# A fused attention and two-layer kernel: the first layer's weights are loaded from ScalarE's queue

## The chip, the cores and the metric

One core of a Trainium2 chip runs the whole program. The metric is the device time of one execution in microseconds (us). The engines are PE (TensorE, matmuls; PEld are its weight loads), DVE (VectorE), ACT (ScalarE), POOL (GpSimd) and SP (SyncE, which here only begins transfers). Each engine works through its own list of instructions in order, and an instruction that waits on a semaphore holds everything behind it on that engine.

## The reference

```python
q_pool = q.reshape(B, H, S // 2, 2, D).mean(axis=3)          # B 4, H 8, S 1152, D 64
scores = q_pool @ k.transpose(0, 1, 3, 2) / sqrt(D)
attn = exp(scores - max(scores)); attn = attn / sum(attn)
x = (attn @ v) as 2304 rows of 512
h = x @ moe_w_in;  x = (h * cos(h)) @ moe_w_out               # 512 to 2048 to 512, weights float64
h = x @ moe2_w_in; out = (h / (1 + exp(-h))) @ moe2_w_out     # the same shapes
```

All inputs and the output are taken as the reference has them: the attention inputs are float32, and the kernel has a way (`wide`) of reading weights whose numbers are eight bytes long.

## The kernel before

The work is cut into 16 pairs of heads: 4 batches, and in each 4 pairs. For a pair, `pair_loads` (L289) begins the transfers of q, k and v, `pair_prep` (L313) finds their largest values (L111, tiles `pm`), makes a scale `ps` from them (L102) and splits each number into a high and a low float16 (L351, L352, L306, L311), and two transposing transfers turn q and k (L357 `qT`, L367 `kT`). A pair has 9 tiles of 128 query rows. Each tile runs `tile_scores` (PE, L391, into the PSUM tiles `sp`), `tile_exp` (DVE L410 reads the scores and their largest value, L415, then ACT L418), `tile_hi` (ACT L424), `tile_lo` (POOL L429, then the transposing transfer `hlT` of L431, 144 of them in the program) and, four tiles later, `tile_pv` (PE, L442 and L446).

The weights of the first layer, `W1`, come in 16 pieces of 1 MB, 8 of `w_in` and 8 of `w_out`, through three buffers named `wst`. `weight_steps` (L155) runs them: `more` (L172) begins a piece's transfer (L177), `decode` (L191) turns the eight-byte numbers into float32 with one ACT instruction (L206, absolute values into `wt`) and four of DVE (L207, L210, L215, L218, of 1024 columns each), then a scale is made as for a pair (L87, L90, L95, L98, L102, L106), and `write` (L232) splits the piece into two float16 halves (ACT L238 and L239, POOL L240) and calls `more` again, which refills the buffer that L240 has just read. The engine that begins the transfers is an argument, `eng`. Three pieces are requested when the generator starts; 13 refills follow.

The second layer's weights, `W2`, go through the same function late in the program (from 925 us in the profile on). The first layer's matmuls (L522, L582) begin after the first batch and run beside the attention of the others; the second layer's (L522, L603) run last, alone.

The order in which the instructions stand on each engine isn't written by hand. The framework places them from the program's order, priorities (`ahead`, `early`) and its own model of when each could run. Each transfer takes the next of eight completion semaphores (DMAHW0 to DMAHW7, in turns over all queues) and waits until that semaphore's last transfer has landed. So a change of a queue moves instructions on every engine.

Of the kernel before, what the change touches and what calls it, by code (L numbers as in the profile page):

```python
# [29 lines left out]
W1_SUB, W1_BUFS, W1_AHEAD, WT_BUFS = 1, 3, 1, 2  # L30
# [14 lines left out]
def attention_moe_moe_kernel(ctx, tc, q, k, v, w_in1, w_out1, w_in2, w_out2, out):  # L45
# [3 lines left out]
    nc = tc.nc  # L49
# [14 lines left out]
    ps_h = ctx.enter_context(tc.tile_pool(name="ps_h", bufs=2, space=PSUM))  # L64
# [56 lines left out]
    def early(g, n):  # L121
        while True:
            with ahead(n):
                r = next(g, END)
            if r is END:
                return
            yield r

    def run_all(g):
        for _ in g:  # L130
            pass
# [13 lines left out]
    def new_w(tag, npc):  # L145
        w = Weights()
        w.npc = npc
        for nm in ("si", "ui", "so", "uo"):
            setattr(w, nm, const.tile([128, npc], F32, name=nm + tag))
        w.uoT = const.tile([128, NC], F32, name="uoT" + tag)  # L150
        w.kg = const.tile([128, 1], F32, name="kg" + tag)
        w.ug = const.tile([128, 1], F32, name="ug" + tag)
        return w
# [122 lines left out]
    def pair_new(at, b, j):  # L276

        P = Pair()  # L280
        P.b, P.j = b, j
        P.on_pool = PREP_POOL if b == 0 else 0
        P.q = at.src.tile([128, 2 * NT + 1, 2, D], F32, tag="stq", name="stq", bufs=1)
        P.k, P.v = (
            [at.src.tile([128, KC, D], F32, tag="stg", name="st" + nm, bufs=NB_S) for i in range(2)] for nm in "kv"
        )
        return P

    def pair_loads(P):  # L289
        heads = (P.j, P.j + NP)  # L290
        n = NT * 128 * 2
        for i, h in enumerate(heads):
            nc.sync.dma_start(
                out=P.q[:, i * NT:(i + 1) * NT], in_=q[P.b, h, 0:n, :].rearrange("(p t r) d -> p t r d", t=NT, r=2)
            )
            nc.sync.dma_start(
                out=P.q[i * 64:(i + 1) * 64, 2 * NT], in_=q[P.b, h, n:, :].rearrange("(p r) d -> p r d", r=2)
            )
            yield
        for src, t in ((k, P.k), (v, P.v)):  # L300
            for i, h in enumerate(heads):
                nc.sync.dma_start(out=t[i], in_=src[P.b, h].rearrange("(p c) d -> p c d", c=KC))
                yield
# [316 lines left out]
    if True:  # L620
        W1 = new_w("1", 8)
# [7 lines left out]
        wst = wst_stack.enter_context(tc.tile_pool(name="wst", bufs=1, reuse_waits="tile"))  # L629
# [66 lines left out]
        for n in range(2):  # L696
            P[n] = pair_new(at, *pairs[n])
            run_all(pair_loads(P[n]))
            if n == 0:
                wg = weight_steps(W1, (w_in1, w_out1), wst, lambda: ps_h, nc.sync, W1_SUB, W1_BUFS, W1_AHEAD)  # L700
                next(wg)
                run_all(pair_prep(at, P[0]))

        def slowly(g, n):
            for _ in g:
                for _ in range(n):
                    yield

        wg = early(slowly(wg, W_PACE), P_W)
# [265 lines left out]
```

## Time and profile before

| | us |
|---|---|
| median of 3 runs | 1421.21 (1418.97 to 1424.5) |
| the profiled execution | 1422.36 |
| its span, first to last instruction | 1420.6 |
| PE busy | 1159.3, 82% |
| DVE busy | 994.6, 70% |
| ACT busy | 774.0, 54% |
| POOL busy | 568.2, 40% |

The shares are averages over stages that differ. A table of busy time by stretch shows a first stage to about 213 us in which DVE is hardly ever idle, a middle one to about 1030 us in which PE and DVE are both between some 75 and 90%, and a last one, to the end, in which PE alone is full. Such a row gives, after the stretch and its length, each engine's busy time with the number of its instructions, then TensorE's granted clock as a share of full speed, the busy share of the 16 DMA engines, and GB/s. In rows of a timeline the columns are start, duration, engine, line, operation, output and inputs, shapes and count; in brackets stands how long the engine was idle just before, and what ended that.

### The profile page before, as it was taken

To read this page: it belongs to the slowest core of one execution; us is meant where nothing else is said; L and a number is where in the kernel's file an instruction comes from. 1 tells how busy PE (TensorE), PEld (TensorE's weight loads), DVE (VectorE), ACT (ScalarE), POOL (GpSimd) and SP (SyncE) were. 2 spreads that over 40 slices of the span, in tenths; PEclk is the share of its full clock that TensorE was granted. 3 is DMA by queue.
4 is the path that set the end of the run, shared out by engine and by line. 5 is a ranking of instruction groups with operands and counts; after the bars stand their busy time and mean duration, and the time that the engine had idled before them with its cause. 6 is when DMAs were issued, how large, how long until landed. Compare 5 with 4: busy or idle time off the path is not lost. (4 is left out here: it accounts for less than half of the span.)

```text
span 1420.6 us, 25141 instructions
## 1 busy us (share of the span) xinstructions
PE 1159.3 (82%) x10020; PEld 850.6 (60%) x10020; DVE 994.6 (70%) x1944; ACT 774.0 (54%) x955; POOL 568.2 (40%) x312
## 2 busy tenths in 40 slices
PE   1465356688888778889889889888799999999998
PEld 0243233476676556667667668677686666666664
DVE  7999997689777898878998976999932322323221
ACT  3686587578677778867779585556611111111110
POOL 1577366545666466645666453354510000000000
PEclk9976578898999989999999999999999999999999
DMA  7799779987799999978999964433210000000000
GB/s 230 191 237 213 184 157 207 204 169 133 143 210 174 204 183 220 191 142 171 177 205 178 201 121 106 123 113 104 75 60 30 23 8 30 30 30 16 16 5 27
DMA packets 493334, 186.19 MB, mean 131 GB/s; under 512 B 433312, under 2 KB 468128, under 8 KB 493216
## 3 DMA queue, kind: packets, MB, share of 16 engines
q1 hardware_dynamic: 493216, 184.59, 61.6%
q8 instruction: 78, 1.28, 0.4%
q14 instruction: 40, 0.33, 0.1%
HBM read 66.58 MB, written 9.44 MB: 54 GB/s over the span
## 5 line engine op out<-in xcount | busy, mean ns | idle before, releaser
L429 POOL TENSOR_TENSOR hl<-sc,hl 128x1152 f16<-128x1152 f32 x144 | 365.5, 2548 | 201.7 <-ACT hl L424 111.7
L391 PE MATMUL sp<-kT,qT 128*128 128x512 f16 (+1 forms) x768 | 191.7, 366 | 111.5 <-DVE sc L410 84.1
L522 PEld LDWEIGHTS <-ih 128*128 128x128 f16 x2304 | 227.4, 100 | 69.0 <-issue 9.7
L535 ACT ACTIVATE hk<-h,ca 128x512 f32<-128x512 f32 x144 | 98.0, 682 | 313.0 <-PE h L522 311.2
L410 DVE TENSOR_SCALAR_CACHE_REDUCE sc<-sp,psu 128x512 f32<-128x512 f32 (+1 forms) x288 | 229.3, 807 | 46.4 <-PE sp L391 40.4
L418 ACT ACTIVATE sc<-sc,nb 128x1152 f32<-128x1152 f32 x144 | 179.8, 1250 | 94.1 <-DVE nb L415 81.1
L442 PE MATMUL pv<-vt,hlT 128*128 128x130 f16 (+1 forms) x1440 | 192.3, 236 | 39.7 <-DMA hlT<-hl 30.7
L522 PE MATMUL h<-ys,ih 128*128 128x256 f16 x1152 | 196.2, 273 | 1.8 <-ACT hk L535 1.8
L522 PE MATMUL h<-xT,ih 128*128 128x256 f16 x1024 | 192.3, 282 | 6.3 <-ACT hk L535 3.1
L442 PEld LDWEIGHTS <-hlT 128*128 128x128 f16 (+1 forms) x1440 | 145.2, 109 | 70.0 <-DMA hlT<-hl 42.7
L446 PE MATMUL pv<-vt,hlT 128*128 128x65 f16 (+1 forms) x1440 | 184.4, 206 | 0.0
L391 PEld LDWEIGHTS <-qT 128*128 128x128 f16 x768 | 76.7, 108 | 174.0 <-issue 130.5
L424 ACT ACTIVATE hl<-sc 128x1152 f16<-128x1152 f32 x144 | 165.2, 1155 | 21.6 <-DMA hlT<-hl 10.8
L570 DVE TENSOR_SCALAR gh<-hk,ck 128x1024 f16<-128x1024 f32 x36 | 27.0, 751 | 207.5 <-PE o L603 193.7
L582 PE MATMUL y<-gh,oh 128*128 128x256 f16 x576 | 159.7, 277 | 4.8 <-ACT y L591 4.8
L582 PE MATMUL y<-gl,oh 128*128 128x256 f16 x576 | 159.7, 277 | 1.5 <-POOL gl L563 1.5
L582 PE MATMUL y<-gh,ol 128*128 128x256 f16 x576 | 159.7, 277 | 0.0
L522 PE MATMUL h<-ys,il 128*128 128x256 f16 x576 | 157.0, 273 | 0.0
L446 PEld LDWEIGHTS <-hlT 128*128 128x128 f16 (+1 forms) x1440 | 140.7, 107 | 15.0 <-issue 6.2
L522 PE MATMUL h<-xT,il 128*128 128x256 f16 x512 | 144.1, 281 | 0.0
L582 PEld LDWEIGHTS <-oh 128*128 128x128 f16 x1152 | 113.8, 100 | 24.5 <-issue 7.4
L522 PEld LDWEIGHTS <-il 128*128 128x128 f16 x1152 | 114.7, 100 | 19.2 <-issue 2.7
(284 smaller groups left out, 2048.6 us busy)
## 6 DMA issues: line engine op xcount, KB each, us to landing
stk<-in_k_dram SPq DMA_DIRECT2D x32, 288.0 KB, 4.1
stv<-in_v_dram SPq DMA_DIRECT2D x32, 288.0 KB, 4.4
stq<-in_q_dram SPq DMA_DIRECT2D x32, 256.0 KB, 3.1
wst<-in_moe_w_in_dram SPq DMA_DIRECT2D x8, 1024.0 KB, 5.9
wst<-in_moe_w_out_dram SPq DMA_DIRECT2D x8, 1024.0 KB, 6.2
wst<-in_moe_w_in_dram SPq DMA_DIRECT2D x16, 512.0 KB, 4.5
wst<-in_moe_w_out_dram SPq DMA_DIRECT2D x16, 512.0 KB, 4.7
ydr<-y SPq DMA_DIRECT2D x9, 512.0 KB, 3.0
```

Of the source, the lines that this page charges most:

```text
L391: nc.tensor.matmul(sp[:, o - a:o - a + n], P.qT[e][:, t, :], kT[:, o:o + n], start=(e == 0), stop=(e == 1))
L410: nc.vector.tensor_scalar(out=T.sc[:, a:z], in0=sp, scalar1=T.P.su, scalar2=None, op0=ALU.mult, op1=ALU.min, accum_out=mx[:, x:x + 1],)
L418: nc.scalar.activation(out=T.sc, in_=T.sc, func=AF.Exp, scale=-1.0, bias=nb)
L424: nc.scalar.activation(out=hi, in_=T.sc, func=AF.Copy)
L429: nc.gpsimd.tensor_tensor(out=T.hl[:, 1, :], in0=T.sc, in1=T.hl[:, 0, :], op=ALU.subtract)
L442: nc.tensor.matmul(G.pv[r, T.gi], T.hlT[:, 0, c, r], P.vt[i][:, c], start=(c == 0), stop=(c == KC - 1), skip_group_check=True,)
L446: nc.tensor.matmul(G.pv[r, T.gi, 0], T.hlT[:, 1, c, r], P.vt[i][:, c, 0], start=False, stop=(c == KC - 1), skip_group_check=True,)
L522: nc.tensor.matmul(hp, wt[:, c, f * 128:(f + 1) * 128], xt(c), start=(i == 0), stop=(i == 3 * NC - 1), skip_group_check=True,)
L535: nc.scalar.activation(out=o, in_=blk.hp, func=AF.Copy if first else AF.Silu, scale=blk.c.a[:, g:g + 1])
L570: nc.vector.tensor_scalar(out=gh, in0=hk, scalar1=blk.c.k, scalar2=None, op0=ALU.mult)
L582: nc.tensor.matmul(blk.y[:, oc, :], wt[:, f, oc * 128:(oc + 1) * 128], gt[:, f % 4, :], start=(f == 0 and e == 0 and oc % 2 == 0), stop=(f ...
```

## The change

The generator of `W1` is given ScalarE's queue in place of SyncE's. All 16 transfers of L177 for `W1` stand on ACT now; the 16 and 16 smaller ones of `W2` and all others stay on SP.

```diff
             if n == 0:
-                wg = weight_steps(W1, (w_in1, w_out1), wst, lambda: ps_h, nc.sync, W1_SUB, W1_BUFS, W1_AHEAD)
+                wg = weight_steps(W1, (w_in1, w_out1), wst, lambda: ps_h, nc.scalar, W1_SUB, W1_BUFS, W1_AHEAD)
                 next(wg)
```

The start of ACT's list, before. `qn`, `kn` and `vt` are the split q, k and v of the first pair, `wst_132`, `wst_134` and `wst_136` the first three weight pieces:

```order
L351 ACT_TABLE_LOAD [waits DMAHW1_49,DMAHW2_49,DMAHW0_49,DMAHW3_49,DVE_49]
L351 ACTIVATE qn_157<-stq_119,ps__148 128x9x64 [waits Pool_49]
L351 ACTIVATE qn_157<-stq_119,ps__148 128x9x64
L306 ACTIVATE kn_164<-stk_120,ps__148 128x9x64 [waits DMAHW4_49]
L306 ACTIVATE kn_164<-stk_121,ps__148 128x9x64 [waits DMAHW5_49]
L306 ACTIVATE vt_171<-stv_122,ps__148 128x9x64 [waits DMAHW6_49]
L306 ACTIVATE vt_176<-stv_123,ps__148 128x9x64 [waits DMAHW7_49]
L206 ACTIVATE wt_215<-wst_132 128x1024 [waits DMAHW0_49]
L206 ACTIVATE wt_234<-wst_134 128x1024 [waits DMAHW1_49]
L206 ACTIVATE wt_276<-wst_136 128x1024 [waits DMAHW2_49,DVE_49]
```

and now:

```order
L177 DMA wst_132<-in_moe_w_in_dram 128x4x512
L177 DMA wst_134<-in_moe_w_in_dram 128x4x512
L177 DMA wst_136<-in_moe_w_in_dram 128x4x512
L206 ACT_TABLE_LOAD
L206 ACTIVATE wt_215<-wst_132 128x1024 [waits DMAHW0_49]
L206 ACTIVATE wt_234<-wst_134 128x1024 [waits DMAHW3_49]
L206 ACTIVATE wt_276<-wst_136 128x1024 [waits DMAHW5_49,DVE_49]
L351 ACTIVATE qn_157<-stq_119,ps__148 128x9x64 [waits DMAHW2_49,DMAHW4_49,DMAHW1_49,DMAHW6_49,DVE_49,Pool_49]
L351 ACTIVATE qn_157<-stq_119,ps__148 128x9x64
L306 ACTIVATE kn_164<-stk_120,ps__148 128x9x64 [waits DMAHW7_49]
```

The three transfers and the three weight instructions L206 have moved ahead of the first pair's instructions.

DVE's list around the first scores (L410 reads `sp`), before:

```order
L90 SCALAR_TENSOR_TENSOR mw_224<-wm_214,mw_224 128x1 [waits DVE_49]
L215 SCALAR_TENSOR_TENSOR wst_134<-wst_134,wt_234 128x1024 [waits DMAHW1_49,DVE_49]
L90 SCALAR_TENSOR_TENSOR mw_261<-wm_233,mw_261 128x1 [waits DVE_49]
L218 SCALAR_TENSOR_TENSOR wst_132<-wst_132 128x1024 [waits DVE_49]
L98 TENSOR_SCALAR ui1_75<-bm_227 128x1 [waits PE_49]
L207 TENSOR_SCALAR wt_276,wm_275<-wt_276 128x1024 [waits Activation_49]
L218 SCALAR_TENSOR_TENSOR wst_134<-wst_134 128x1024 [waits DVE_49]
L98 TENSOR_SCALAR ui1_75<-bm_264 128x1 [waits PE_49]
L102 TENSOR_SCALAR si1_74<-ui1_75 128x1 [waits DVE_49]
L410 TENSOR_SCALAR sc_202,mx_203<-sp_194,psu_155 128x512 [waits PE_49]
```

and now:

```order
L102 TENSOR_SCALAR si1_74<-ui1_75 128x1 [waits DVE_49]
L355 COPY qn_157<-qn_157 128x9x64 [waits DVE_49]
L106 TENSOR_SCALAR ui1_75<-ui1_75 128x1 [waits DVE_49]
L311 SCALAR_TENSOR_TENSOR kn_164<-stk_120,ps__148,kn_164 128x9x64 [waits Activation_49]
L311 SCALAR_TENSOR_TENSOR kn_164<-stk_121,ps__148,kn_164 128x9x64 [waits Activation_49]
L311 SCALAR_TENSOR_TENSOR vt_171<-stv_122,ps__148,vt_171 128x9x64 [waits Activation_49]
L311 SCALAR_TENSOR_TENSOR vt_176<-stv_123,ps__148,vt_176 128x9x64 [waits Activation_49]
L410 TENSOR_SCALAR sc_202,mx_203<-sp_194,psu_155 128x512 [waits PE_49]
L410 TENSOR_SCALAR sc_202,mx_203<-sp_195,psu_155 128x640 [waits PE_49]
L111 TENSOR_REDUCE pm_220<-stk_183 128x1 [waits DMAHW2_49]
L410 TENSOR_SCALAR sc_246,mx_247<-sp_238,psu_155 128x512 [waits PE_49]
L415 TENSOR_SCALAR nb_206<-mx_203 128x1 [waits DVE_49]
```

All three pieces are decoded ahead of the first pair's split now (in before the third piece's L210, L215 and L218 stand behind the first L410), and nothing stands between the split of v (`vt`) and the first L410. Up to the first L410 the list has one L210, one L215, one L218 and eight instructions of 1 to 3 columns more than before. From the fourth L207 on the two lists have the weights and the score tiles in nearly the same mixture; from the 535th of DVE's 1610 instructions (376 us in the profile of before) to the 1254th they are alike, row for row.

ACT's list in the middle of the first stage, before. `oh` is the high half of a piece of `w_out`, L206 opens the next piece:

```order
L239 ACTIVATE wst_650<-wst_650,so1_76 128x1024 [waits Activation_49]
L206 ACTIVATE wt_867<-wst_802 128x1024 [waits DMAHW0_49]
L238 ACTIVATE oh1_83<-wst_728,so1_76 128x16x64 [waits DVE_49]
L239 ACTIVATE wst_728<-wst_728,so1_76 128x1024 [waits Activation_49,Pool_49]
L465 ACTIVATE x32_575<-pvs_1515,den_1512 128x64 [waits DVE_49]
L465 ACTIVATE x32_576<-pvs_1515,den_1512 128x64 x2
L238 ACTIVATE oh1_83<-wst_802,so1_76 128x16x64 [waits DVE_49]
```

and now:

```order
L238 ACTIVATE oh1_83<-wst_650,so1_76 128x16x64 [waits DVE_49]
L177 DMA wst_802<-in_moe_w_out_dram 128x16x128 [waits Pool_49]
L239 ACTIVATE wst_650<-wst_650,so1_76 128x1024 [waits Activation_49]
L238 ACTIVATE oh1_83<-wst_728,so1_76 128x16x64 [waits DVE_49]
L206 ACTIVATE wt_867<-wst_802 128x1024 [waits DMAHW1_49]
L177 DMA wst_863<-in_moe_w_out_dram 128x16x128 [waits Pool_49]
L239 ACTIVATE wst_728<-wst_728,so1_76 128x1024 [waits Activation_49]
L177 DMA wst_923<-in_moe_w_out_dram 128x16x128 [waits Pool_49]
L206 ACTIVATE wt_933<-wst_863 128x1024 [waits DMAHW3_49]
```

Each refill stands on ACT behind the L239 of some piece and waits on POOL's L240; where two follow each other closely, as here, ACT's L206 for the next piece stands behind them. On SP the refills are gone, and the pair's loads and transposes follow each other.

Before the third pair's first L410 DVE's list has the same shape: behind the split of k (`kn`) stand the split of v and two weight pieces' instructions, of L207 one fewer than before.

## Rows read from the trace of the kernel before

**Rows 1.** Busy time by stretch: us, PE, PEld, DVE, ACT, POOL, clock, DMA share, GB/s.

```profile
0.00:35.50 35.50, 5.94 (x18) 2.92 (x18) 25.26 (x52) 13.28 (x14) 5.55 (x15) 1.00 0.78 230
...
71.00:106.50 35.50, 21.95 (x186) 14.69 (x185) 35.35 (x77) 29.47 (x32) 25.52 (x12) 0.71 1.11 237
...
35.50:213.00 177.50, 88.21 (x688) 57.61 (x688) 172.32 (x345) 123.40 (x136) 105.78 (x52) 0.73 0.89 196
213.00:284.00 71.00, 46.04 (x437) 29.77 (x438) 48.66 (x129) 46.74 (x54) 43.00 (x25) 0.84 1.09 206
...
960.00:1030.00 70.00, 57.36 (x488) 48.99 (x488) 66.68 (x130) 43.68 (x68) 34.45 (x20) 0.95 0.30 91
```

**Rows 2.** DVE's timeline, start of the program to the first scores.

```profile
7.27 0.75 DVE L111 TENSOR_REDUCE pm<-stk 128x1 f32<-128x576 f32 x1 [6.27 <-DMA stk<-in_k_dram]
...
12.30 0.17 DVE L102 TENSOR_SCALAR ps__148<-pu__149 128x3 int32<-128x3 int32 x1
...
18.98 1.22 DVE L207 TENSOR_SCALAR_CACHE_REDUCE wt<-wt 128x1024 f32<-128x1024 f32 x1
...
22.59 0.68 DVE L210 TENSOR_SCALAR wt<-wt 128x1024 int32<-128x1024 int32 x1
...
23.26 1.22 DVE L215 SCALAR_TENSOR_TENSOR wst<-wst,wt 128x1024 int32<-128x1024 int32 x1
...
25.66 1.22 DVE L218 SCALAR_TENSOR_TENSOR wst<-wst 128x1024 int32<-128x1024 int32 x1
...
29.58 0.74 DVE L410 TENSOR_SCALAR_CACHE_REDUCE sc<-sp,psu 128x512 f32<-128x512 f32 x1
```

**Rows 3.** Timelines of SP, ACT and PE in the same stretch.

```profile
0.74 0.40 SPq L293 DMA_DIRECT2D stq<-in_q_dram  x1
...
16.06 3.94 SPq L357 DMA_TRANSPOSE qT<-qn  x1
20.11 2.69 SPq L367 DMA_TRANSPOSE kT<-kn  x1
...
12.54 1.28 ACT L351 ACT_TABLE_LOAD   x1 [12.54 <-DVE ps__148 L102]
...
17.84 2.13 ACT L206 ACTIVATE wt<-wst 128x1024 f32<-128x1024 f32 x2
...
26.25 2.08 PE L391 MATMUL sp<-kT,qT 128*128 128x512 f16 x6
```

**Rows 4.** Weight pieces, issue to landing: the first three, then all 16 of `W1`.

```profile
DMA to landing us min/median/max: 8.1/10.3/12.4
...
DMA to landing us min/median/max: 5.2/6.1/12.4
```

**Rows 5.** Instructions on the tile `wst` to 213 us: ns min/median/max, first and last start.

```profile
L177 SPq DMA_DIRECT2D wst<-in_moe_w_out_dram x8: 367/523/692, 93.4 to 178.5; - x8
...
L240 POOL TENSOR_TENSOR il<-wst,ih x8: 2129/2224/3109, 32.2 to 118.8; 128x1024 f16<-128x1024 f32 x8
```

**Rows 6.** The transposing transfers of L431 to 213 us, in the same columns.

```profile
L431 SPq DMA_TRANSPOSE hlT<-hl x24: 2486/2782/5341, 44.4 to 202.1; - x24
```

**Rows 7.** DVE's groups by shape to 376 us: busy us, mean ns | idle before.

```profile
L215 DVE SCALAR_TENSOR_TENSOR wst<-wst,wt 128x1024 int32<-128x1024 int32 x16 | 30.4, 1898 | 0.0
L218 DVE SCALAR_TENSOR_TENSOR wst<-wst 128x1024 int32<-128x1024 int32 x16 | 27.7, 1729 | 0.0
L210 DVE TENSOR_SCALAR wt<-wt 128x1024 int32<-128x1024 int32 x16 | 21.0, 1313 | 0.0
```

**Rows 8.** DVE's waits from 213 to 284 us: total, times, longest.

```profile
DVE sc L410 <- PE sp L391: 14.3, 9, 5.2
```

**Rows 9.** DVE's timeline at the third pair's first scores.

```profile
152.27 0.32 DVE L355 COPY qn<-qn 128x576 f16<-128x576 f16 x1
...
163.07 0.74 DVE L410 TENSOR_SCALAR_CACHE_REDUCE sc<-sp,psu 128x512 f32<-128x512 f32 x1
```

**Rows 10.** Transfers by line: count, median us from issue to landing.

```profile
kT<-kn SPq DMA_TRANSPOSE x16, 4.8
```

## The prediction

> **What bounds the kernel now.** I read busy time by stretch first [rows 1]. From 35.5 to 213 us DVE works 172.32 of 177.5 us, so it is idle for only 5.2 us: while all weights of the first layer are decoded and the first batch's attention runs, DVE sets the pace. ACT is busy for 123.4 us there and has 54.1 to spare; in the tightest stretch, 71 to 106.5 us, it has 6.0. From 213 to 284 us DVE is busy for 48.66 of 71 us, and most of its idle time, 14.3 us, ends with PE's scores [rows 8]. What DVE has lost by 213 us comes later for everybody, since the scores, exponentials and transposes of the later tiles hang on DVE's list, and that list is the same in both kernels from 376 to about 914 us. The change is in the first stage, so the question is when DVE reaches the end of that stage.
>
> The start is the second view [rows 2, 3]. DVE begins at 7.27 us with the largest values of the first pair, has the scale `ps` at 12.30 to 12.47, and takes the first scores at 29.58. Between the split of the pair and those scores it decodes two and a half weight pieces, and that is what hides the transposes of q and k and the first matmuls.
>
> **The start, the main term.** The order shows that DVE now decodes all three pieces before it splits the first pair. Step by step:
>
> - The first piece's transfer can begin at 0.74 us, when SP begins its first [rows 3]. One megabyte took 8.1 to 12.4 us behind the pair's loads, and 5.2 at best with less beside it [rows 4]. ACT's three issues aren't in the trace; SP's took 0.37 to 0.69 us each [rows 5]. I take the middle of 5.2 and 8.1, 6.65, since the first pair's loads run beside it, and so 7.4 us for the landing (5.9 to 8.8). One L206 follows, 1.1 us (half of 2.13 [rows 3]); ACT's table load falls into the wait. DVE starts at 8.5 us (7.0 to 9.9).
> - Ahead of the scale `ps` it then has three each of L207 (1.22), L210 (0.68), L215 (1.22) and L218 (1.22) and six L111 (0.75) [rows 2]: 13.0 + 4.5 = 17.5 us, and a dozen small ones that about make up for the 0.07 us by which starts overlap. `ps` stands at 26.0 us (24.5 to 27.4).
> - From `ps` to the first scores: before, `ps` ended at 12.47, PE began the scores at 26.25 and had the first half about 1 us later, 14.8 us in all [rows 2, 3]. Three things shorten that. The table load of 1.28 us sat in this chain and is now paid earlier. The q transpose took 3.94 us beside the weight loads, the k transpose 2.69 [rows 3]: 1.25 less. And k had landed by 24.9 us (20.11 + 4.8 [rows 3, 10]), while PE waited until 26.25 behind two small matmuls of the weights: 1.3 less. All three give 11.0, none 14.8. I take 11.5, nearest to all three. The first L410 comes at 37.5 us.
> - By then DVE has done more than before: one L210, L215 and L218 and eight tiny ones, 0.68 + 1.22 + 1.22 + 0.4 = 3.5 us. The loss is 37.5 - 29.58 - 3.5 = 4.4 us; the ends give 24.5 + 11.0 - 33.1 = 2.4 and 27.4 + 14.8 - 33.1 = 9.1.
>
> In plain words: DVE used to split the pair first and decode while the transposes ran. Now it decodes first and then stands still, about 6 us, for the transposes. Earlier weights buy nothing, because DVE had weight work in hand at every moment from 18.98 us on.
>
> **The third pair, a small second term.** From `kn` to the third pair's first scores the list has one L207 less. Before, 10.5 us lay between L355's end and that L410, without a wait [rows 9]. The chain of q transpose, k transpose and first matmuls takes about 2.7 + 4.8 + 1.0 = 8.5 us [rows 3, 10], and DVE's own work there is now 10.5 less 1.22, or less 3 where POOL holds it up less: 7.5 to 9.3. I take 1.0 us (0 to 2.5).
>
> **ACT's queue, 13 refills.** Their issue costs ACT 13 x 0.52 = 6.8 us by SP's median [rows 5]. Each also waits for POOL's L240, 2.2 us [rows 5], where it stands close behind the L239 that feeds it. ACT's 54.1 idle us cover both, since four score buffers let DVE run ahead of ACT; the tight stretch has 6.0 us for two or three refills. I take 0.5 us (0 to 18, the first rival below). Two table loads fewer in the program, 1.28 us each on ACT, are covered in the same way: 0. SP loses 13 issues and its waits for weight buffers; in this stage DVE waits for none of SP's transfers for long, so 0.
>
> The Trainium skill speaks against a gain from a second queue: "DMA: Bandwidth & Descriptors", section "Issuing engines are not separate DMA queues", says that transfers begun by different engines run on the same 16 DMA engines and interleave, so that a second issuer saves issue time only. By that alone the sum would be zero, 1421 us; no row of before has a second issuer to test it.
>
> **Meetings with POOL, no direction.** L215, L218 and L210 take 1.90, 1.73 and 1.31 us on average [rows 7], and 1.22, 1.22 and 0.68 at the start, where POOL does nothing [rows 2]. That is 16 x (0.68 + 0.51 + 0.63) = 29 us of the stage, spent where they meet POOL's subtractions. The first three pieces meet none in either order; the other 13 keep nearly the same mixture with the tiles. I take 0 and give it 8 us to either side, about a quarter of the 29.
>
> **The second layer's weights.** From 960 to 1030 us DVE is busy for 66.68 of 70 us [rows 1], and its list differs in a few places there, with the same work. 0, within 3 us.
>
> **Sum.** 4.4 + 1.0 + 0.5 = about 6 us. The profiled execution took 1422.36 us, 1.15 above the median of 1421.21, so its terms carry over: 1428.3 for an execution like it, 1427.2 against the median.
>
> **The rivals.** A measurement of this kernel can tell about 0.5% from no change, 7.1 us.
>
> - *ACT becomes the bound, slower.* SP spends 2.78 us on each transpose [rows 6] and 13 refills fall among 24 of them. If ACT can't begin a transfer while SP is in one, and meets one each time, a refill costs 0.52 + 2.78 + 2.22 = 5.5 us and 13 cost 72, 18 more than the 54.1 that ACT has: 1421.2 + 6 + 18 = 1445. It decides from an average of 4.2 us per refill (54.1 / 13). Against it: 24 transposes fill 67 of 177.5 us, so most refills should meet none, and POOL is often done by then. The Trainium skill, "Perfetto Trace Analysis", section "DMA Instruction — HWDGE (DVE, Sync)", has a rule that would do this: the descriptor generator is locked for one instruction at a time, and the profiled duration includes the wait for the lock. No row of before shows two issuers. Chance 0.12.
> - *The start at its dear end, slower.* The landing at 8.8 us, nothing saved between `ps` and the scores, and the third pair's 2.5: 9.1 + 2.5 = 11.6, so 1433. It passes 7.1 already when the start costs 6 instead of 4.4, or POOL adds 2. Chance 0.29.
> - *Nothing is lost.* The first piece lands early and the transposes run fast, or DVE's later waits for scores (14.3 us [rows 8]) swallow a delay: 1421 to 1423. Chance 0.15.
> - *The decode meets POOL less, faster.* Half of the 29 us saved: 6 - 14.5 = -8.5, so 1412.7. For it: while DVE stood still, POOL and ACT got ahead, so later meetings shift. Against it: nothing in the order makes them fewer. Chance 0.11.
>
> **How the numbers follow.** The forecast, 1427 us, has a chance of 0.33; with "nothing is lost" that makes 0.48 for within 0.5%. Slower by more is 0.29 + 0.12 = 0.41, faster by more 0.11. The range goes from the middle of the faster case, 1413, to 1441, most of the way to the ACT rival: below it lies half of the 0.11, above it most of the 0.12.
>
> **What would show it.** In the profile of the changed kernel DVE should start with L207 near 8.5 us, `ps` should come near 26, DVE should be idle for about 6 us before the first L410, near 37.5, and the gap to before should still be there at 213 us. ACT's L177 should take about half a microsecond; 3 us and more beside SP's transposes would mean the ACT rival, and long waits of L418 or L206 behind L177 with DVE idle would go with it. The forecast is wrong if DVE has its first scores before 33 us, if the mean of L215 and L218 moves by over 0.3 us, or if the gap at 213 us is gone by 376.

## The result and the profile after

The changed kernel took 1431.34 us (median of 7 runs, 1428.08 to 1433.14) and the kernel before 1424.50 in the same comparison (7 runs, 1418.97 to 1427.98). The ratio is 1.0052, with a 95% interval of 1.0037 to 1.0068: a loss of about 7 us, where the sum of the prediction's terms was 6. The profiled execution of the changed kernel is the median one (span 1429.5). The one of before, 1422.36, lies 2.1 us under its own median of 7, so the two traces differ by 9 us, and some 2 of them are the luck of one run.

The forecast was 1427.2 us, counted from a median of 1421.21 before; of the 4.1 us that are missing in it, 3.3 come from that median, which is higher in these 7 runs.

Busy time by stretch after, in the columns of [rows 1]:

```profile
0.00:35.50 35.50, 2.19 (x8) 2.04 (x9) 23.26 (x50) 13.49 (x15) 2.29 (x14) 1.00 0.59 182
35.50:213.00 177.50, 92.96 (x698) 57.69 (x697) 167.85 (x341) 118.11 (x129) 101.36 (x52) 0.64 0.90 200
213.00:284.00 71.00, 42.15 (x388) 25.57 (x389) 48.85 (x130) 48.90 (x58) 43.50 (x25) 0.78 1.11 202
960.00:1030.00 70.00, 57.84 (x488) 48.82 (x486) 70.00 (x142) 42.27 (x66) 35.58 (x19) 0.95 0.40 119
```

In the first 35.5 us DVE has worked 2 us less than before, and in the next 177.5 us it is idle for 9.65 us where it was idle for 5.2. ACT has more time to spare than before, not less. TensorE's granted clock is lower from 35.5 to 213 us (0.64 of full speed where it was 0.73, a mixture of its levels of 1.2 and 2.4 GHz) while PE is busy for 92.96 us where it was 88.21. No run tells the clock apart from the rest, but from 45 to 215 us DVE waits for PE's scores for 1.9 us where it waited for 0.4, so these waits leave the clock some 1.5 us of the gap there. DVE's timeline at the start answers [rows 2]:

```profile
7.90 1.22 DVE L207 TENSOR_SCALAR_CACHE_REDUCE wt<-wt 128x1024 f32<-128x1024 f32 x1 [6.89 <-ACT wt L206]
...
26.44 0.16 DVE L102 TENSOR_SCALAR ps__148<-pu__149 128x3 int32<-128x3 int32 x1
...
38.04 0.75 DVE L410 TENSOR_SCALAR_CACHE_REDUCE sc<-sp,psu 128x512 f32<-128x512 f32 x1 [6.20 <-PE sp L391]
```

The timelines of ACT, SP and PE in the same stretch answer [rows 3]:

```profile
0.73 1.63 ACTq L177 DMA_DIRECT2D wst<-in_moe_w_in_dram  x3
2.39 1.28 ACT L206 ACT_TABLE_LOAD   x1 [2.39 <-issue]
...
28.90 3.38 SPq L357 DMA_TRANSPOSE qT<-qn  x1
32.32 2.91 SPq L367 DMA_TRANSPOSE kT<-kn  x1
...
36.99 2.93 PE L391 MATMUL sp<-kT,qT 128*128 128x512 f16 x8 [9.62 <-DMA kT<-kn]
```

DVE begins with a weight piece, has `ps` 14 us later than before, and then stands for 6.20 us until PE, which itself stood for the transpose of k, has the first scores. The decode groups of [rows 7], to 376 us, have changed too:

```profile
L218 DVE SCALAR_TENSOR_TENSOR wst<-wst 128x1024 int32<-128x1024 int32 x16 | 24.2, 1515 | 0.0
L210 DVE TENSOR_SCALAR wt<-wt 128x1024 int32<-128x1024 int32 x16 | 23.6, 1476 | 0.1
L215 DVE SCALAR_TENSOR_TENSOR wst<-wst,wt 128x1024 int32<-128x1024 int32 x16 | 23.0, 1437 | 0.1
```

Together they take 70.8 us where they took 79.1. To see what that is worth, DVE's whole timeline was summed in both traces between places of its list up to which both have done the same instructions (reads of the accumulator aside, and at the 388th but for one L111):

| up to DVE's | ends before, after (us) | gap | of it idle time, busy time added since the line above |
|---|---|---|---|
| 193rd instruction | 127.3, 129.5 | 2.1 | +7.0, -4.9 |
| 279th | 181.2, 189.7 | 8.5 | +2.2, +4.2 |
| 388th | 259.7, 265.0 | 5.3 | +1.3, -4.5 |
| 528th | 368.2, 377.8 | 9.5 | -1.3, +5.5 |
| 1253rd | 913.9, 923.6 | 9.7 | -4.3, +4.4 |
| last, the 1608th | 1415.7, 1425.1 | 9.4 | -5.5, +5.1 |

Up to the 528th instruction DVE's busy time differs by 0.3 us and its idle time by 9.2. What the decode saved, other instructions that met POOL took. So the loss is idle time of the first stage, and nothing gives it back. This division holds for the first stage only: behind the 528th instruction DVE's busy time grows by 9.5 us and its idle time shrinks by 9.8, while the gap stays.

### The profile page after: what moved, and what is told of

It is laid out like the page before. It is cut to its first block, busy times and chain, and to the rows that moved or that the text cites. A ratio compares the mean times of both kernels' runs of the same rounds, so it can differ in the third digit from the quotient of the medians.

```text
span 1429.5 us, 25125 instructions
## 1 busy us (share of the span) xinstructions
PE 1165.8 (82%) x10020; PEld 852.7 (60%) x10020; DVE 1004.5 (70%) x1944; ACT 773.1 (54%) x953; POOL 569.0 (40%) x312
## 3 DMA queue, kind: packets, MB, share of 16 engines
q8 instruction: 78, 1.28, 0.4%
## 5 line engine op out<-in xcount | busy, mean ns | idle before, releaser
L410 DVE TENSOR_SCALAR_CACHE_REDUCE sc<-sp,psu 128x512 f32<-128x512 f32 (+1 forms) x288 | 229.3, 807 | 54.0 <-PE sp L391 48.8
L570 DVE TENSOR_SCALAR gh<-hk,ck 128x1024 f16<-128x1024 f32 x36 | 27.0, 751 | 202.3 <-PE o L603 197.9
L563 POOL TENSOR_TENSOR gl<-tt,gh 128x1024 f16<-128x1024 f32 x36 | 93.7, 2604 | 88.7 <-DVE gh L562 66.6
```

Of the source, the lines that this page charges most:

```text
L410: nc.vector.tensor_scalar(out=T.sc[:, a:z], in0=sp, scalar1=T.P.su, scalar2=None, op0=ALU.mult, op1=ALU.min, accum_out=mx[:, x:x + 1],)
L563: nc.gpsimd.tensor_tensor(out=G.gl, in0=t, in1=gh, op=ALU.subtract)
```

## The experiments: one part at a time

The first three kernels begin a part of the transfers on ACT, the fourth none. The framework is free to place all other instructions anew, as it was in the change itself.

Only the first three on ACT, the 13 refills on SP (`eng` is changed when the first three have been requested):

```diff
         for _ in range(bufs):
             more()
-        yield
+        eng = nc.sync if w is W1 else eng; yield
...
-                wg = weight_steps(W1, (w_in1, w_out1), wst, lambda: ps_h, nc.sync, W1_SUB, W1_BUFS, W1_AHEAD)
+                wg = weight_steps(W1, (w_in1, w_out1), wst, lambda: ps_h, nc.scalar, W1_SUB, W1_BUFS, W1_AHEAD)
```

> The first three transfers of W1 on ACT as in the changed kernel, the 13 refills back on SP. Theory A (the start: DVE decodes three pieces before it splits the first pair, then stands still for the transposes) expects the loss whole: ps near 26.5 us, an idle stretch of about 6 us before the first L410 near 38, 12 to 17 us of DVE idle to 45 us, and 5 to 8 us more than before in the median. Theory B (the refills on ACT's queue hold ACT and with it the decode) expects 0 to 2 us more than before. Theory C (any new mixture of weight pieces and score tiles shifts how often DVE's decode meets POOL's subtractions) expects the same start as A, but a total that can lie 5 us to either side of it, with the mean of L215, L218 and L210 telling which.

Measured: ratio 1.0035 (1.0020 to 1.0050), 5 us more than before; `ps` near 26.6, first scores at 38.26, DVE idle for 16.1 us to 45 us. Theory A holds for this part.

Only the refills on ACT:

```diff
-        yield
+        eng = nc.scalar if w is W1 else eng; yield
```

> The first three transfers of W1 on SP as before, the 13 refills on ACT. Theory A (the start) expects a start as before, first L410 at 29.6 us, and a median within 2 us of before. Theory B (the refills on ACT's queue) expects the 5 to 7 us of the changed kernel, with L177 on ACT or ACT's waits behind it as the cause. Theory C (the mixture) expects a start as before and a total that moves by up to 5 us either way with the means of L215, L218 and L210.

Measured: ratio 1.0037 (1.0018 to 1.0056), 5 us more, though the start is that of before (first scores at 28.89). Theory A alone is not enough. ACT's timeline shows one way in which the refills cost in the order that this kernel got:

```profile
138.81 1.23 ACT L238 ACTIVATE oh<-wst,so 128x1024 f16<-128x1024 f32 x1 [6.06 <-DVE so L102]
138.81 0.38 ACTq L177 DMA_DIRECT2D wst<-in_moe_w_out_dram  x1
...
147.65 1.12 ACT L206 ACTIVATE wt<-wst 128x1024 f32<-128x1024 f32 x1 [3.30 <-DMA wst<-in_moe_w_out_dram]
147.66 2.54 ACTq L177 DMA_DIRECT2D wst<-in_moe_w_out_dram  x2
```

POOL had left that buffer at 134.8 us, but the refill stands behind L238, and L238 waited for DVE. The piece lands 9 us after its issue, and DVE's timeline has the bill:

```profile
148.80 1.22 DVE L207 TENSOR_SCALAR_CACHE_REDUCE wt<-wt 128x1024 f32<-128x1024 f32 x1 [7.74 <-ACT wt L206]
```

All on ACT, but the first three held back until the first pair's k has landed:

```diff
+                if w is W1 and len(todo) >= 13: nc.gpsimd.tensor_copy(st.bitcast(F32)[:, 0, 0, 0:1], P[0].k[0][:, 0, 0:1])
                 eng.dma_start(
```

> All 16 transfers of W1 on ACT, but each of the first three waits for POOL to have copied one column of the first pair's k into its buffer, so that the pieces land after the pair's loads, as before. Nothing else is changed, and the order puts the split of the first pair ahead of the decode again. Theory A (the start) expects ps near 12.5 us, the first L410 near 29.6, and a median within 2 us of before: the whole loss is undone though every transfer stands on ACT. Theory B (ACT's queue) expects 5 to 7 us more than before. Theory C (the mixture) expects up to 5 us to either side of before.

Measured: ratio 1.0066 (1.0045 to 1.0087), 9 us more. The start is even better than that of before (first scores at 26.83, a lead of 4.7 us at the 36th L410), and at the 37th, the third pair's first, the lead is gone and DVE is 8.3 us behind before. DVE's waits from 100 to 215 us have one row:

```profile
DVE wt L207 <- ACT wt L206: 8.5, 3, 4.7
```

The framework's order has the 15th piece ahead of the third pair's first scores here, and DVE stands for it. So a good start alone saves nothing, and theory A as the whole cause has fallen.

All on SP, but the first three requested ahead of the first pair's loads:

```diff
             P[n] = pair_new(at, *pairs[n])
+            if n == 0:
+                wg = weight_steps(W1, (w_in1, w_out1), wst, lambda: ps_h, nc.sync, W1_SUB, W1_BUFS, W1_AHEAD)
+                next(wg)
             run_all(pair_loads(P[n]))
             if n == 0:
-                wg = weight_steps(W1, (w_in1, w_out1), wst, lambda: ps_h, nc.sync, W1_SUB, W1_BUFS, W1_AHEAD)
-                next(wg)
                 run_all(pair_prep(at, P[0]))
```

> All transfers on SP as before, but the first three weight pieces are requested ahead of the first pair's loads, so that the order decodes them first, as the changed kernel does. Theory A (the start) expects the changed kernel's loss without its queue: idle of 6 us before the first L410 near 38 to 40 us and 5 to 9 us more than before. Theory B (ACT's queue) expects no loss beyond the pair's loads standing 1.5 us later on SP: 0 to 2 us. Theory C (the mixture) expects A's start and up to 5 us to either side of A's total.

Measured: ratio 1.0012 (0.9996 to 1.0029), 2 us more, with the first scores at 35.94 and 14.8 us of idle time to 45 us. The same start in kind, 2 us shorter than after, costs less than A said.

Each of these also gets a new order, so none of them tells a queue from an order. The next kernels do.

## The experiments: the order held

Here each engine's instructions are kept in the row in which another kernel has them. Only the weight transfers in question are free. It takes edges that order the issue without a wait, added when the program has been traced (`_ORDER` lists, engine by engine, the places that the instructions have in the traced program):

```python
    dep = mybir.DependencyInfo(mybir.DependencyClass.NoSync, mybir.DependencyReason.SCHED_ONLY)
    ...
        for x, y in zip(row, row[1:]):
            tc.add_manual_dep(ins[y], ins[x].name, dep, reason="order")
```

The changed kernel in the order of before:

```diff
-                wg = weight_steps(W1, (w_in1, w_out1), wst, lambda: ps_h, nc.sync, W1_SUB, W1_BUFS, W1_AHEAD)
+                wg = weight_steps(W1, (w_in1, w_out1), wst, lambda: ps_h, nc.scalar, W1_SUB, W1_BUFS, W1_AHEAD)
...
-        attention_moe_moe_kernel(tc, *args)
+        attention_moe_moe_kernel(tc, *args); keep_order(tc)
```

> The changed kernel (all 16 transfers of W1 on ACT), but the other instructions of DVE, ACT, POOL, PE and SP are held in the row in which they stand in the kernel before; only the 16 transfers are new in ACT's row and gone from SP's. Theory Q (the loss is ACT's queue: refills that stand behind ACT's waits, transfers that meet SP's) expects 5 to 8 us more than before. Theory O (the loss is the order that the framework makes of it) expects a median within 2 us of before, or up to 3 us less, since SP's transposes no longer stand behind weight transfers; first L410 at 27 to 30 us, DVE idle 8 to 11 us to 45 us and under 3 us waiting for L206 between 100 and 180.

Measured: ratio 1.0085 (1.0061 to 1.0108), 12 us more. The order of before does not save the change. DVE's timeline says why at the start (in before the same L111 began at 7.27, [rows 2]):

```profile
10.94 0.75 DVE L111 TENSOR_REDUCE pm<-stk 128x1 f32<-128x576 f32 x1 [9.94 <-DMA stk<-in_k_dram]
...
34.69 0.73 DVE L410 TENSOR_SCALAR_CACHE_REDUCE sc<-sp,psu 128x512 f32<-128x512 f32 x1
```

Three megabytes of weights, begun at 0.7 us, now travel ahead of and beside the first pair's loads, and k lands 3.7 us later. That is not all sharing of the DMA engines. SP's waits to 40 us, its loads of v before, and the same here:

```profile
SPq L302 <- DMA wst<-in_moe_w_in_dram: 5.8, 2, 3.0
...
4.08 0.91 SPq L302 DMA_DIRECT2D stv<-in_v_dram  x2
...
7.29 0.91 SPq L302 DMA_DIRECT2D stv<-in_v_dram  x2
```

SP's second load of k takes the completion semaphore of ACT's first piece and stands for 2.8 of these 5.8 us until that piece has landed, and the loads of v, behind it, are begun 3.2 us later. The scale `ps` comes at 17.71 us, 5.4 later than before, and the first scores 5.1 later. So the early pieces cost in either order: DVE decodes first and waits for transposes, or splits first and waits for k.

The kernel before in the order of the changed one (the only edit is `keep_order`, with the other list):

> The kernel before (all transfers on SP), but the other instructions of DVE, ACT, POOL, PE and SP are held in the row in which they stand in the changed kernel; only the 16 transfers have gone from ACT's row back into SP's. Theory Q (ACT's queue) expects a median within 2 us of before. Theory O (the order) expects the changed kernel's loss, 5 to 9 us, and its marks: first L410 near 38 us with about 6 us of DVE idle before it, the third pair's first scores near 172 to 176 us.

Measured: ratio 1.0066 (1.0042 to 1.0091), 9 us more. On SP the pieces land later, and an order that begins with them waits longer, first for the piece and then again for the scores:

```profile
14.93 1.22 DVE L207 TENSOR_SCALAR_CACHE_REDUCE wt<-wt 128x1024 f32<-128x1024 f32 x1 [13.93 <-ACT wt L206]
...
43.60 0.75 DVE L410 TENSOR_SCALAR_CACHE_REDUCE sc<-sp,psu 128x512 f32<-128x512 f32 x1 [6.43 <-PE sp L391]
```

Theory O's size is met, and its 6 us of idle time before the first scores, but these come 5.6 us later than its 38. Neither Q nor O is the whole cause.

The order of before, all on ACT, the first three held back by k:

> As the kernel in which the first three transfers on ACT wait until the first pair's k has landed (POOL copies one column of k into each buffer), but with every other instruction held in the row in which it stands in the kernel before. Theory Q expects 5 to 8 us more than before. Theory O expects the lead that this start had at 121 us (4.7 us in the profile of that kernel) to be kept: 2 to 5 us less than before, with the first L410 near 27 us and the third pair's first scores near 159.

Measured: ratio 1.0013 (0.9995 to 1.0031), 2 us more. Beside the first kernel of this section it differs in the holding back alone: the first scores come 7.7 us earlier (26.99), and the median is 11 us lower. That is the price of early pieces in this order, but for some 1.3 us: with the pieces held back, ACT loads its table while it has nothing else to do (further down). But it starts 2.6 us ahead of before and doesn't end ahead: in the same order of instructions, 5 to 8 us are lost between 140 and 215 us. That made a new theory, R: the refills of a second queue share the 16 DMA engines with SP's transfers and delay those that somebody waits for. Its rival S: a row made for one timing of the transfers loses under any other. Three kernels test them.

The order of the changed kernel, first three on ACT, refills back on SP:

> The changed kernel with its first three transfers on ACT and its 13 refills back on SP, every other instruction of all engines held in the row of the changed kernel. Theory R (two separate costs: the start, and refills of a second queue that share the DMA engines with SP's transposes) expects the changed kernel's start (first L410 near 38 us) and 0 to 4 us less than the changed kernel, so 3 to 7 us more than before. Theory S (a row made for one timing of the transfers loses under any other timing) expects 2 to 6 us more than the changed kernel, so 9 to 13 us more than before.

Measured: ratio 1.0035 (1.0021 to 1.0049), 5 us more than before and 2.4 less than the changed kernel, with its start (first scores at 38.14 after 6.16 us of idle time). R's range is met and S's is not. But the intervals of this kernel and the changed one overlap, so the 2.4 us are not clear of noise.

The order of before, only the refills on ACT:

> The kernel before with only its 13 refills on ACT, every other instruction of all engines held in the row of the kernel before. Theory R expects the start of before (first L410 at 29 to 30 us) and then the loss that the gated kernel showed between 140 and 215 us (transposes hlT that land late beside a refill, DVE waiting 3 to 4 us for L454 near 148): 2 to 6 us more than before. Theory S expects 5 to 10 us more. If the refills cost nothing in this row, 0 to 1 us.

Measured: ratio 1.0072 (1.0046 to 1.0097), 10 us more: over what R gave, and at the upper end of S's 5 to 10. DVE's waits from 60 to 215 us:

```profile
DVE den L454 <- PE pv L446: 4.2, 2, 3.6
DVE sc L410 <- PE sp L391: 3.2, 3, 2.0
DVE pm L111 <- POOL stq L316: 2.6, 1, 2.6
```

In before the first is 0.6 us, the second 0.4, and the third isn't there. The transfers explain the first and the third. In before, the issues and landings (median us) of 138 to 142 us, and of the fourth pair's q from 155 to 172 us:

```profile
q1 hardware_dynamic: 3054, 0.78, 105.5%
...
hlT<-hl SPq DMA_TRANSPOSE x2, 4.6
...
stq<-in_q_dram SPq DMA_DIRECT2D x1, 256.0 KB, 3.0
```

The same with the refills on ACT (with the queues' packets, MB and share from 142 to 150 us ahead of the last line):

```profile
wst<-in_moe_w_out_dram ACTq DMA_DIRECT2D x1, 1024.0 KB, 9.6
hlT<-hl SPq DMA_TRANSPOSE x2, 7.7
...
q10 hardware_dynamic: 2064, 1.05, 57.8%
q1 hardware_dynamic: 964, 0.24, 17.4%
...
stq<-in_q_dram SPq DMA_DIRECT2D x1, 256.0 KB, 6.3
```

SP's queue is q1, ACT's q10. On SP the refill stood behind both transposes and behind q's loads and took nothing from them. On ACT it is served between their packets: the transposes' median is 7.7 us instead of 4.6 (of the two, the later one landed 9.5 us after its issue instead of 4.7), PE waits for it, and DVE for PE.

The pieces held back by k, but the refills on SP, in the order of before:

```diff
-        yield
+        eng = nc.sync if w is W1 else eng; yield
```

> The first three transfers on ACT and gated by the first pair's k, the 13 refills on SP, every other instruction held in the row of the kernel before. Theory R expects the lead of 2.6 us at the first L410 (near 27 us) to be kept, since nothing shares the DMA engines with SP's transposes: 1 to 4 us less than before. Theory S expects 2 to 5 us more than before.

Measured: ratio 0.9986 (0.9967 to 1.0005), median 1420.56 against 1423.53. The lead holds this time: first scores at 27.68, and DVE is about 2 to 4 us ahead of before from the 10th L410 (51 us) to the 78th (255 us) and 3.3 at the last L570, though it falls to nothing for a time between. S's 2 to 5 us more has fallen. DVE's waits from 60 to 215 us have the transposes' wait at its old size:

```profile
DVE den L454 <- PE pv L446: 0.6, 1, 0.6
```

This is the only version that lies under the kernel before, by 2 to 3 us; the interval just reaches no change, so it isn't shown to be faster. Nor is its lead one of transfers: k lands 0.1 us earlier than before (the first L111 at 7.15). DVE's split of q before, then ACT's table load and DVE's split of q here:

```profile
14.64 0.82 DVE L352 SCALAR_TENSOR_TENSOR qn<-stq,ps__148,qn 128x576 f16<-128x576 f32 x1 [1.72 <-ACT qn L351]
...
9.02 1.28 ACT L351 ACT_TABLE_LOAD   x1 [9.02 <-issue]
...
12.68 0.82 DVE L352 SCALAR_TENSOR_TENSOR qn<-stq,ps__151,qn 128x576 f16<-128x576 f32 x1 [0.39 <-ACT qn L351]
```

Before, the table load of 1.28 us began when `ps` was there, at 12.54 us [rows 3], and DVE waited for it. Here it is done ahead of `ps`. That is 1.3 of the 1.9 us by which the first scores come earlier.

Last, the refills divided by what R holds against them. Two of the 13 on ACT, those beside the two transposes and beside q:

```diff
-                eng.dma_start(
+                (nc.scalar if w is W1 and len(todo) in (3, 1) else eng).dma_start(
```

> The kernel before with only two of its 16 transfers on ACT, the 13th and the 15th piece (in the kernel with all refills on ACT these are the two that lie beside the last two transposes hlT of the second pair, near 140 us, and beside the fourth pair's q, near 161), everything else held in the row of the kernel before. Theory R (a second queue's refill takes its share of the DMA engines from transfers of SP that are waited for) expects DVE's waits of 3 to 4 us for L454 near 150 and of 2 to 3 us for L111 of stq near 170 to come back, and 3 to 6 us more than before. Theory S (any refill on ACT loses a little) expects 2/13 of the loss of all refills, about 1 us, and no such waits.

Measured: ratio 1.0032 (1.0017 to 1.0046), 4.6 us more. DVE's waits from 60 to 215 us:

```profile
DVE pm L111 <- POOL stq L316: 2.5, 1, 2.5
DVE den L454 <- PE pv L446: 2.4, 2, 1.8
```

Both waits are back, the longest for L454 at half its size, and two transfers cost nearly half of what 13 do. S, which means here that any refill loses a little, gave them 1 us and has fallen for these two. The other eleven on ACT (`len(todo) < 13 and len(todo) not in (3, 1)`):

> The complement: the 13th and 15th piece on SP as before, the other 11 refills on ACT, everything else held in the row of the kernel before. Theory R expects no wait for L454 near 150 and none for L111 of stq near 170, but still the wait of 2 us for scores near 84 us: 1 to 4 us more than before. Theory S expects 11/13 of the loss of all refills, 6 to 9 us more.

Measured: ratio 1.0040 (1.0016 to 1.0063), 5.7 us more. R's 1 to 4 is missed and S's 6 to 9 nearly met, and the interval (2 to 9 us) reaches into both, so this run doesn't decide between them. There is a wait of 3.1 us for `stq` that R did not expect. SP's timeline shows where it is from:

```profile
164.54 0.38 SPq L177 DMA_DIRECT2D wst<-in_moe_w_out_dram  x1
164.96 1.95 SPq L296 DMA_DIRECT2D stq<-in_q_dram  x1
```

In before the refill is begun behind this last load of q. Here the framework put it one place ahead, since the place of the transfers was left free. One place on the same queue brings a wait of the size that the second queue brought (2.6): for this load it is a question of which transfer goes first. How much of the 5.7 us the eleven would cost without this is open.

## Why the prediction came out as it did

- *What bounds the kernel.* Right: DVE's list in the first stage sets the pace, and what is lost there comes later for everybody. The gap of 9.5 us at the 528th instruction is 9.4 at the last, and DVE's wait for scores from 213 to 284 us did not swallow it, 14.2 us where [rows 8] had 14.3, at the same busy time (48.85 and 48.66 us). That ends the rival in which nothing is lost.
- *The start.* Right step by step: L207 was forecast for 8.5 us and came at 7.90, `ps` for 26.0 and 26.44, 11.5 us from there to the scores and 11.4, first scores for 37.5 and 38.04, about 6 us of idle time and 6.20. The loss of 4.4 us was 38.04 - 29.58 - 3.5 = 5.0 in the trace, and 5 us, clear of noise, in the two kernels that have this start with refills on SP. In the third, with its first scores at 35.94, the same sum gives 2.9, and 2 were measured.
- *Earlier weights buy nothing.* Right, but half of it: the held order showed a cost that the prediction did not count, the first pair's k landing 3.7 us later and the loads behind it waiting for ACT's piece. In the changed kernel the order hides it behind the decode.
- *The third pair.* The size was at the upper end (idle time of 2.2 us more from the 193rd to the 279th instruction, in a range of 0 to 2.5), but the forecast chain is not what made it. DVE's waits from 45 to 215 us:

```profile
DVE wt L207 <- ACT wt L206: 2.1, 1, 2.1
DVE sc L410 <- PE sp L391: 1.9, 3, 1.1
```

  The wait for L206 was not in the prediction, and it is not the queue's:

```profile
147.41 1.20 ACT L238 ACTIVATE oh<-wst,so 128x1024 f16<-128x1024 f32 x1 [4.18 <-DVE so L102]
...
148.51 1.10 ACT L206 ACTIVATE wt<-wst 128x1024 f32<-128x1024 f32 x1
```

  In ACT's row L206 stands behind the L238 of an earlier piece, and that waits for a scale from DVE; then DVE waits for both. The two kernels that hold this row with refills on SP have the same wait of 2.1 us, so it belongs to the order. The wait of 1.1 us is at the third pair's first scores, as forecast, but not from the chain in its usual length. The transpose of k, the matmuls behind it and those scores, and then the first two in the kernel with the same row and its refills on SP:

```profile
166.00 2.81 SPq L367 DMA_TRANSPOSE kT<-kn  x1
...
173.47 2.08 PE L391 MATMUL sp<-kT,qT 128*128 128x512 f16 x6 [12.81 <-DMA kT<-kn]
...
174.52 0.75 DVE L410 TENSOR_SCALAR_CACHE_REDUCE sc<-sp,psu 128x512 f32<-128x512 f32 x1 [1.14 <-PE sp L391]
...
163.64 2.84 SPq L367 DMA_TRANSPOSE kT<-kn  x1
...
168.26 2.08 PE L391 MATMUL sp<-kT,qT 128*128 128x512 f16 x6 [9.79 <-DMA kT<-kn]
```

  In the changed kernel ACT begins a refill at 167.71 us, 1.7 us behind this transpose, which lands 7.4 us after its issue; with the refill behind it on SP it takes 4.6, and DVE doesn't wait at these scores. So the second queue shows in the changed kernel itself.
- *ACT's queue, 13 refills.* The term was too small and its mechanism wrong. 0.5 us (0 to 18) was worked out from ACT's idle time. ACT has that time, and L177 takes it as little as forecast:

```profile
L177 ACTq DMA_DIRECT2D wst<-in_moe_w_in_dram x8: 374/388/573, 0.7 to 89.6; - x8
...
L177 ACTq DMA_DIRECT2D wst<-in_moe_w_out_dram x8: 374/374/498, 97.8 to 170.3; - x8
```

  But refills on ACT cost 2.4 us in the new order (not clear of noise), 4 between the two kernels with the first pieces held back (1.0013 and 0.9986), and 5 and 10 in the two that moved the refills alone, by two ways that the prediction did not name: a refill behind an ACT instruction that waits for DVE goes out late, which the trace of one order of the framework's shows, and a refill that goes out early takes DMA time from SP's transposes and loads, which the changed kernel's shows too. "SP loses 13 issues, so 0" looked at SP's time and not at the row in which its transfers were served.
- *ACT becomes the bound.* It fell as forecast: no L177 in this kernel takes over 0.6 us, while the lock of the Trainium skill ("Perfetto Trace Analysis", section "DMA Instruction — HWDGE (DVE, Sync)") would have shown as 2.8 us and more beside a transpose. None of its 16 issues shows such a wait; the one at 167.71 us took 0.38, inside SP's issue of a transpose from 166.00 to 168.81.
- *The page against a second queue.* The Trainium skill, "DMA: Bandwidth & Descriptors", section "Issuing engines are not separate DMA queues", says that transfers of different engines interleave on the same DMA engines. The trace agrees (q1 and q10 in one stretch, landings of 7.7 us instead of 4.6). The reading of it as "the sum is zero" was wrong: interleaving is a loss where the order of one queue was a good one.
- *Meetings with POOL.* The sum was right, at 0 (busy time 0.3 us more by the 528th instruction), and the test that was named for it was a bad one: the mean of L215 moved by 0.46 us, beyond the 0.3 that was to refute the forecast, while other rows took the time back. The row to watch is all of DVE's busy time between like places.
- *The second layer's weights.* 0, as forecast, though not at every moment: from 960 to 1030 us DVE is busy for all 70 us, the gap grows to 12.5 us there, and it is back at 9.4 at the end, after 9.7 at the 1253rd instruction.

What stays open: how much of the loss is the lower clock of TensorE, if any. The kernel with only its refills on ACT has runs from 1424.89 to 1438.29, and its trace is of the fastest, so the trace shows 3 of the 10 us that the median lost. And how the loss of the changed kernel divides is known to some 2 us each, by intervals of that width: 5 us with the start and the refills on SP, whether the row is held or not, and 2.4, which may be 0, for the refills on ACT.

## What to carry to other kernels

Moving transfers to another engine's queue moves their issue, their rank among all transfers, the completion semaphores that transfers of other queues take turns with, and, where a framework orders the program, every engine's list. Ask of each transfer who waits for it and what stood behind it in the old queue, because one queue is an order of service that a second queue dissolves. To tell a queue from an order, hold the order and move the transfers, and the other way round; and compare DVE's idle and busy time only between places where both lists have done the same work.

## What the runs showed of the hardware that was not expected

- A 1 MB transfer on a second queue, begun within a microsecond of a transposing transfer on the first, raised the median landing of that transpose and the one ahead of it from 4.6 to 7.7 us (its own from 4.7 to 9.5) and took 9.6 us itself, where such a piece takes 6.2 (the median for `w_out` in before, from 40 to 213 us).
- The rank matters within one queue, too: a load of q behind a weight piece was issued in 1.95 us instead of 0.47, and DVE waited 3.1 us for it.
- Three weight pieces begun from ACT at 0.7 us delayed k, begun from SP at about 3.5 us, by 3.7 us: it took 3.1 us longer to land and was begun 0.5 later. SP's second load of k stood for 2.8 us until the first piece on ACT had landed, whose completion semaphore it takes.
- ACT's table load of 1.28 us began at 12.54 us, behind `ps`, in the kernel before, and at 9.02, ahead of it, in the last kernel with its first pieces held back. DVE's wait for the split of q went from 1.72 to 0.39 us.
- No issue of ACT waited for one of SP: one of 0.38 us lies inside SP's issue of a transpose of 2.81 us.
